# Low words of the weights and the residual, added by accumulating transfers instead of VectorE

## The chip, the cores and the metric

The kernel runs on one core of a Trainium2 chip. Its engines are TensorE (matrix products, in the profile PE, its weight loads PEld), VectorE (DVE), ScalarE (ACT), GpSimd (POOL) and SyncE (SP), which here only issues transfers. The metric is the device time of one execution in microseconds. Lower is better.

## The reference

There are 4 batches of 1088 positions, with 4 heads of 32 channels. The first part is an attention with a feature map instead of a softmax: two small projections a = S1 x and b = S2 x of 8 channels each, whose 64 products are the features.

```python
def phi(x):
    a = np.einsum('rd,bhsd->bhsr', S1, x)
    b = np.einsum('rd,bhsd->bhsr', S2, x)
    return np.einsum('bhsi,bhsj->bhsij', a, b).reshape(*x.shape[:-1], r * r)
q_p, k_p = phi(q), phi(k)
kv = np.einsum('bhsf,bhsd->bhfd', k_p, v)
z = np.sum(k_p, axis=2)
out = np.einsum('bhsf,bhfd->bhsd', q_p, kv) / (np.einsum('bhsf,bhf->bhs', q_p, z)[..., None] + 1e-6)
```

Its output, with the heads side by side, is x (4 x 1088 x 128). The second part is a gated feed-forward layer, in which a 1088 x 1088 matrix w_sg mixes the positions:

```python
h = gelu_tanh(x @ w_in)                # 128 -> 1024
u, v = h[..., :512], h[..., 512:]
v_n = (v - mean(v)) / sqrt(var(v) + 1e-6) * g_ln
v_s = np.einsum('ts,bsd->btd', w_sg, v_n) + b_sg[None, :, None]
return x + (u * v_s) @ w_out           # 512 -> 128, and the residual x
```

## The kernel before

**Words.** Most products run on float32r operands. An operand is split into a high word (its copy to float32r) and a low word (the operand less its high word), and a product is three matmuls: high with high, low with high, high with low. The names end in h and l: w_h and w_l are the words of w_sg, xh and xl those of x, ar holds both words of the normalised v, win, wout, gh/gl and kvt likewise. Line 806 makes the low words of w_sg: `V.tensor_sub(w_l[t][r], w_f[t][r], f32(w_h[r, t]))`, with w_f the loaded fp32 tile and w_h made from it by ScalarE (line 798).

**Tiles.** w_sg (transposed) lies in nine tiles of 128 input positions by 1088 output positions; the last has 64 rows. The outputs are taken in three chunks (CH) of 362, 362 and 364 columns. The 512 channels are four blocks (db) of 128. Tile t of w_l is put into the buffer of w_f tile t - 1, which must then have been read by all; the first has a spare one.

**The head** (class Head) does the attention of batch 0, its first layer, the normalisation and the mixing of its first channel block with unsplit fp32 weights (line 792), by an order written out in HEAD. Of its steps `wlo` is left out; the nine subtractions are tasks of the planner, each behind the last one.

**Behind the head** everything is a task of the class Plan: engine, assumed duration, what it reads and writes, which buffer it takes and frees, and, for TensorE, a position (`pos`). `late` is the time that the planner puts between the end of a task and the start of those that use it on another engine; a transfer of SP has a term for its size. Plan.order then lays the tasks out: always the task that can start first, among equals the one with the earliest due time, where due times come from TensorE's positions. The instructions are issued in this order, so each engine's queue, SP's and GpSimd's too, is worked through in an order fixed beforehand. UNITS, OUTS and SIDE hold the positions of the tasks that are not in the main line of matmuls.

**The stages.** After the head, batch 0's block 1 is mixed by two passes over the nine tiles, the first with w_h (lines 1348, 1350), the second with w_l (line 1346), while batch 1's attention (function attention) fills in. Blocks 2 and 3 follow (function standard). Batches 1 to 3 use a scheme with fewer products (function pair, lines 992 to 994 and 1003, 1004), which needs four weight combinations for the middle chunk. The function combine makes them once: it loads pieces of w_sg to tmp, adds and splits them on VectorE and ScalarE, and puts them into the DRAM buffer td; the plain words of tiles 4 to 7 go there too (lines 1029 and 1031, from w_h and w_l). The function stream loads them from td into w_h and w_l when they are due (lines 1064 and 1066).

**Transfers.** Nearly all are issued by SP, in the planner's order; a transfer that has to wait holds those behind it in the queue. The attention of a batch sends its projected q through the DRAM buffer dq (lines 1120, 1127, 1130) to spread it over partitions into ea and eb, loads k, v and q (1074, 1073, 1108), and VectorE multiplies ea with eb (line 1133).

**GpSimd** computes the inverse deviations of the normalisation (rest_g, lines 389 to 399), on which ScalarE waits to scale v (line 407), and fills a few constants, among them the lower half of the last w_l tile (line 805).

**The residual.** The function store closes a chunk of a batch: VectorE adds x's high word to the PSUM sum (line 960) and then x's low word (line 962), and SP stores the chunk (line 963). Batch 3 has a way of its own (line 958 and the function finish).

Of the kernel before, what the change touches and what calls it, by code (L numbers as in the profile page):

```python
# [9 lines left out]
F32 = mybir.dt.float32  # L10
F32R = mybir.dt.float32r
# [3 lines left out]
ALU = mybir.AluOpType  # L15
PSUM = bass.MemoryType.PSUM

B, H, S, D, R = 4, 4, 1088, 32, 8
P = 128
NT = 9  # L20
SP = NT * P
C = H * D
# [13 lines left out]
STARTS = (0.0, 96.0, 166.0, 236.0)  # L36
SIDE = [
    dict(
        k=[-69.5, -129.7, -258.62, 75.49, -16.81, -86.04, 99.22, -240.4, 467.74],
        m=[44.69, -2.17, -319.74, 128.68, -11.47, -380.37, -268.7, -327.69, -223.35],  # L40
        q=[-500.43, 26.57, 6.61],
        n=[-114.19, -31.31, 54.44, 107.92, 21.3, 18.55],
        v=[79.56, 57.62, 53.21, 95.41, 35.99, 315.99, 135.47, 134.1, 132.66],
    ),
    dict(
        k=[218.33, 108.5, 326.21, 556.29, 74.57, 349.63, 133.75, 142.17, 225.9],
        m=[152.43, 77.78, 138.8, 126.37, 195.45, 192.13, 317.54, 192.52, 217.9],
        q=[180.4, 148.25, 224.71],
        n=[84, 60.63, 131.2, 152.41, 137.24, 137.3],
        v=[281.37, 122.55, 229.64, 134.94, 133.73, 377.89, 212.58, 231.54, 221.6],  # L50
    ),
    dict(
        k=[713.88, 618.5, 144.7, 446.47, 381.41, 661.37, 485.59, 592.49, 451.01],
        m=[544.76, 607.03, 749.31, 502.75, 435.58, 443.92, 701.5, 703.57, 650.71],
        q=[226.39, 486.87, 752.47],
        n=[331.16, 423.26, 232.12, 454.36, 318.97, 567.45],
        v=[174.62, 186.57, 195.46, 166.87, 182.54, 154.59, 170.58, 189.58, 182.28],
    ),
]
UNITS = [  # L60
    [-875.2, 12.55, 557.21],
    [2.71, 22.55, -216.57],
    [18.91, -70.82, -27.37],
    [-13.89, 13.83, 7.58],
    [279.85, -10.36, 44.7],
    [94.74, -5.75, 123.14],
    [707.44, 198.02, 352.81],
    [-16.87, 201.58, -1.1],
    [-37.3, 24.54, -11.45],
    [11.79, 635.2, 58.72],  # L70
    [-11.47, 344.92, 228.92],
    [3.94, 15.41, -20.81],
    [341.58, 228.07, 273.13],
    [213.33, -23.55, 35.18],
    [28.54, -43.91, 111.65],
    [61.61, 4.4, 340.75],
]
OUTS = [
    [12.14, 10.35, 36.95],
    [30.29, -7.66, -11.46],  # L80
    [20.16, -4.85, 29.52],
    [31.06, 7.15, 8.98],
    [-4.83, 12.03, 9.94],
    [6.46, 68.4, 12.69],
    [531.54, 460.78, 293.13],
    [-11.57, 77.49, 47.42],
    [-31.49, 49.03, -30.53],
    [59.58, -26.68, -27.79],
    [986.46, 99.38, 1064.04],
    [211.11, 37.91, 512.89],  # L90
    [7.13, 23.51, 4.52],
    [197.69, 92.31, 345.68],
    [264.01, 186.46, 4.38],
    [1.55, 384.4, 4.5],
]
HEAD = [
# [20 lines left out]
def f32(ap):  # L117
    return ap.bitcast(F32)
# [14 lines left out]
class Plan:  # L133
# [9 lines left out]
    def add(self, eng, dur, f, r=(), w=(), take=(), free=(), pos=None, late=None, start=None, after=(), kb=0):  # L143
        n = len(self.tasks)
        take = dict(take)
        r, w = list(r), list(w) + list(take)
        deps = set(after)
        for k in r + w:
            if k in self.wrote:
                deps.add(self.wrote[k])  # L150
        for k in w:
            deps.update(self.read.pop(k, ()))
        for k in w:
            self.wrote[k] = n
        for k in r:
            if k not in w:
                self.read.setdefault(k, []).append(n)
        deps.discard(n)
        late = (2.3 + kb / 300 if eng == "SP" else self.LATE.get(eng, 0)) if late is None else late
        self.tasks.append(dict(eng=eng, dur=dur, f=f, deps=deps, take=take, free=list(free), pos=pos, late=late, start=start, kb=kb))  # L160
        return n
# [94 lines left out]
def tile_kernel(ctx: ExitStack, tc: tile.TileContext, qd, kd, vd, sd, wd, bd, wind, gd, woutd, identd, outd):  # L256
    nc = tc.nc
    mm = nc.tensor.matmul
    V, A, G = nc.vector, nc.scalar, nc.gpsimd
    load = nc.sync.dma_start  # L260

    cpool = ctx.enter_context(tc.tile_pool(name="const", bufs=1))
    dram = ctx.enter_context(tc.tile_pool(name="dram", bufs=1, space=bass.MemoryType.DRAM))
# [37 lines left out]
    wpool = Pool(ctx.enter_context(tc.tile_pool(name="w", bufs=1)), 1, w=NT + 1)  # L301
    w_f, w_l = {}, {}
# [159 lines left out]
    class Head:  # L462
# [7 lines left out]
        def load(self, name, ns, f, after=()):  # L470
            self.s.at(name, "SP", 0.47, f, after, late=-ns)
# [347 lines left out]
    def xtiles(b, xp):  # L819
        return [xp.tile([P, SP], F32R, name=f"x{b % 2}_{i}", tag=f"x{b % 2}_{i}") for i in "hl"]  # L820

    xp0 = ctx.enter_context(tc.tile_pool(name="x0", bufs=1))
    xs = [xtiles(0, xp0)]
    g = Gate(0, xs[0])
    with tc.tile_pool(name="stage", bufs=1) as stp:
        head = Head(Pool(stp, 1, wst=2, kb0=2, den=2, bst=2, nv=3, ny=3, nh=3, np=3), xs[0], g)
# [14 lines left out]
    pot = [None] * 3  # L841

    plan = Plan(dict(ps=3, gt=NG, u=NU, gh=NH, gl=NL))
    add, got = plan.add, plan.got
    dv = lambda n: 0.075 + n * 1.04e-3
    ac = lambda n: 0.09 + n * 0.83e-3
    pe = lambda n: 0.005 + n * 0.443e-3

    def load_(_, kb, f, **kw):
        return add("SP", 0.47, f, kb=kb, **kw)  # L850
# [13 lines left out]
    def gt(k):  # L864
        return gtt[plan.got[k]]
# [14 lines left out]

    for c in range(3):
        add(None, 0, None, w=[("po", c)], start=START["PE"])
    for t in range(NT):
        lo = add("V", 1.29, head.s.steps["wlo", t][2], w=[("w", t, c, 1) for c in range(3)], after=[lo] if t else [])
    done_lo = lo

    clock = [0.0]

# [9 lines left out]
    def unit(b, q):  # L898
        db, ci = q
        c0, cw = CH[ci]  # L900
        k = ("pu", b, q)
        xh, xl = xs[b % 2]

        def f():
            o, cs, ws = ps(k)[:, :cw], slice(c0, c0 + cw), slice(P * db, P * db + P)
            mm(o, lhsT=win_h[:, ws], rhs=xh[:, cs], start=True, stop=False)  # L906
            mm(o, lhsT=win_l[:, ws], rhs=xh[:, cs], start=False, stop=False)  # L907
            mm(o, lhsT=win_h[:, ws], rhs=xl[:, cs], start=False, stop=True)  # L908

        pemain(3 * pe(cw), f, UNITS[4 * b + db][ci], r=[("win",)] + [("x", b % 2, c) for c in range(3)], take={k: "ps"})  # L910
        u = ("u", b, q)
        add("A", 0.05 + ac(cw), lambda: A.activation(utt[plan.got[u]][:, :cw], ps(k)[:, :cw], AF.Gelu_apprx_tanh),  # L912
            r=[k], take={u: "u"}, free=[k])
# [38 lines left out]
    def store(b, ci):  # L952
        c0, cw = CH[ci]
        cs = slice(c0, c0 + cw)
        xh, xl = xs[b % 2]
        k = ("o", b, ci)
        if b == B - 1:
            add("V", 0.06 + dv(cw), lambda: V.tensor_add(gt(k)[:, :cw], pot[ci][:, :cw], xf(ci)[:, :cw]), r=[("po", ci), ("xf", ci)], take={k: "gt"})
        else:
            add("V", 0.06 + dv(cw), lambda: V.tensor_add(gt(k)[:, :cw], pot[ci][:, :cw], f32(xh[:, cs])),  # L960
                r=[("po", ci)] + [("x", b % 2, c) for c in range(3)], take={k: "gt"})
            add("V", dv(cw), lambda: V.tensor_add(gt(k)[:, :cw], gt(k)[:, :cw], f32(xl[:, cs])), r=[("x", b % 2, c) for c in range(3)], w=[k])
        load_("", 186, lambda: load(outd[b, :, cs], gt(k)[:, :cw]), r=[k], free=[k])


    def words(dst, q, key, r, n=512):
# [102 lines left out]
    def attention(b):  # L1069
        xh, xl = xs[b % 2]  # L1070
# [34 lines left out]
        for ci, (c0, cw) in enumerate(CA):  # L1105
            cs = slice(c0, c0 + cw)
# [56 lines left out]
            if ci == 2:  # L1163
                for x in (xh, xl):
                    add("V", dv(64), lambda x=x: V.tensor_copy(x[:, S:SP], f32(x[:, S - 64 : S])), w=[xk])

        g = gates[b] = Gate(b, xs[b % 2])
        waste = kpt[2].bitcast(mybir.dt.bfloat16)
        s1 = slot(b, 1)
# [130 lines left out]
    def xf(ci):  # L1300
        if "x" not in now:
            now["x"] = here("r0")
        return now["x"][:, ci] if ci < 2 else now["r2"]
# [23 lines left out]

    add("A", 0.1, lambda: A.mul(ng_col, g_col, -1.0), w=["ng"])
    add("G", 0.1, lambda: G.memset(now["r2"][:, 360:], 1.0), w=[("r", 2, 0), ("r", 2, 1)])

    unit(0, (1, 0))
    for ci in range(3):
# [4 lines left out]
    for i in range(2 * NT):  # L1337
        t, low = i % NT, i >= NT
        for ci in range(3):
            cw = CH[ci][1]  # L1340
# [11 lines left out]
            k = dict(take={"z12": "ps"}) if ci == 2 and i == 0 else dict(w=[zks[ci]])  # L1352
            pemain((1 if low or t == 8 else 2) * pe(cw), f, r=[("ar", t // 4) if t < 8 else ("rs", 0)] + [("w", t, ci, 1)] * low, **k)
        if i in (9, 11, 13):
            q = units.pop(0)
# [6 lines left out]
    for ci in range(3):  # L1362
        evac(0, (1, ci), zs[ci], zks[ci], g_col, free=["z12"] if ci == 2 else ())
        if ci:
            unit(0, (1, ci))
        gate(0, (1, ci))
    attention(1)
    for ci in (0, 1, 2):
        standard(0, 2, ci, ci % 2, (2, 3), 1)
# [11 lines left out]
    for b in range(1, B):  # L1381
        clock[0] = STARTS[b]
        if b == B - 1:
            before_end(b)
        pair(b, 0, e, zi)
        if b + 1 < B:
            attention(b + 1)
        pair(b, 1, e, 1 - zi)
# [38 lines left out]
```

## Time and profile before

| | |
|---|---|
| time, median of 3 runs | 348.51 us (346.77 to 349.98) |
| profiled execution | 347.09 us |
| its span, first to last instruction | 345.3 us |
| mean granted TensorE clock | 0.996 |
| busy PE / DVE / ACT / POOL | 332.4 / 271.4 / 217.7 / 23.0 us |
| moved by DMA | 68.87 MB, mean 199 GB/s |

A time is that of the whole execution; the span and all times of single instructions are those of the one profiled execution, counted from its first instruction. A row of a group of instructions gives line, engine, operation, output and inputs, shape, count, then busy us, mean ns of one, and the idle time of the engine ahead of them with what ended it. A row of waits gives who waited for whom, the total in us, how often, and the longest. The matmuls overlap, so TensorE counts as busy in gaps shorter than a matmul's own latency.

### The profile page before, as it was taken

Reading aid. Unit: us, or ns where it says so; the run is one execution under the profiler, and the core shown is the slowest. Engines: PE = TensorE matmul, PEld = TensorE weight load, DVE = VectorE, ACT = ScalarE, POOL = GpSimd, SP = SyncE. Lnnn points to the kernel's source line nnn. Section 1 sums busy time; section 2 is a strip of 40 time slices with the busy share of each in tenths; the row PEclk is TensorE's granted clock in tenths of the full one; section 3 lists DMA queues with packets and bytes.
Section 4 is the critical chain, followed back from the end, with each engine's and each line's share of the span. In section 5 each row is a group of like instructions: output and inputs, shape, how many; then the busy total and the mean of one; then the engine's idle time right before and its main releaser. Section 6 shows DMA issues by size and latency. Waiting matters only on the chain.

```text
span 345.3 us, 5940 instructions
## 1 busy us (share of the span) xinstructions
PE 332.4 (96%) x1952; PEld 311.4 (90%) x1952; DVE 271.4 (79%) x619; ACT 217.7 (63%) x517; POOL 23.0 (7%) x86
## 2 busy tenths in 40 slices
PE   8998999999999979999999999999999999999995
PEld 7876559998999869889999999999999999999994
DVE  4798999998997598979973989989647765874764
ACT  5476862464579989637659986658979644332331
POOL 0002000000000330000002400000006000000000
PEclk9999999999999999999999999999999999999998
DMA  7996033566567755899996854784509905874601
GB/s 246 392 393 219 7 104 99 151 203 192 164 189 253 211 158 151 269 276 325 265 282 196 271 153 132 210 284 152 172 19 317 348 7 173 289 272 136 210 26 62
DMA packets 56175, 68.87 MB, mean 199 GB/s; under 512 B 5008, under 2 KB 53456, under 8 KB 56144
## 3 DMA queue, kind: packets, MB, share of 16 engines
q1 hardware_dynamic: 56000, 68.40, 63.2%
q8 instruction: 15, 0.25, 0.3%
q14 instruction: 16, 0.13, 0.1%
q10 hardware_dynamic: 144, 0.09, 0.1%
HBM read 59.48 MB, written 8.99 MB: 198 GB/s over the span
## 4 chain that ended last, share of the span: by engine, by line
PE 70%; DMA 13%; DVE 11%; issue 2%; ACT 2%; SPq 1%; DVEq 0%
PE bz L992 12%; PE bz L993 11%; PE bz L994 11%; DMA eb<-dq 4%; DMA td<-tmp 3%; PE pz L792 3%; PE bs L1091 2%; PE pab L668 2%; DMA tmp<-in_w 2%; DMA w_h<-td 2%; PE bs L906 2%; PE bs L907 2%; PE bs L908 2%; PE bz L1004 2%; PE bz L1003 2%
## 5 line engine op out<-in xcount | busy, mean ns | idle before, releaser
L992 PE MATMUL bz<-w_h,ar 128*128 128x362 f32 (+1 forms) x288 | 95.6, 332 | 1.9 <-DMA w_h<-td 1.3
L993 PE MATMUL bz<-w_h,ar 128*128 128x362 f32 (+1 forms) x288 | 94.7, 329 | 0.2 <-DVE ar L968 0.2
L994 PE MATMUL bz<-w_l,ar 128*128 128x362 f32 (+1 forms) x288 | 94.7, 329 | 0.0
L992 PEld LDWEIGHTS bz<-w_h,ar 128*128 128x128 f32 x288 | 54.3, 188 | 3.7 <-DMA w_h<-td 1.7
L993 PEld LDWEIGHTS bz<-w_h,ar 128*128 128x128 f32 x288 | 54.2, 188 | 1.0 <-DVE ar L968 0.5
L994 PEld LDWEIGHTS bz<-w_l,ar 128*128 128x128 f32 x288 | 54.2, 188 | 0.0
L967 ACT CAST ar<-vn 128x512 fp32r<-128x512 f32 x40 | 24.7, 620 | 23.1 <-PE bz L994 21.9
L936 ACT CAST gh<-gt 128x362 fp32r<-128x362 f32 (+1 forms) x47 | 23.1, 496 | 21.7 <-DVE gt L935 10.9
L968 DVE TENSOR_TENSOR ar<-vn,ar 128x512 fp32r<-128x512 f32 x40 | 27.3, 684 | 8.0 <-ACT ar L967 7.8
L912 ACT ACTIVATE u<-bs 128x362 f32<-128x362 f32 (+1 forms) x48 | 22.4, 470 | 15.4 <-PE bs L908 7.6
L937 DVE TENSOR_TENSOR gl<-gt,gh 128x362 fp32r<-128x362 f32 (+1 forms) x47 | 24.6, 532 | 6.7 <-ACT gh L936 6.6
L407 ACT ACTIVATE vn<-vn,st 128x512 f32<-128x512 f32 x36 | 27.7, 815 | 2.9 <-POOL st L538 2.3
L935 DVE TENSOR_TENSOR gt<-gt,u 128x362 f32<-128x362 f32 (+1 forms) x47 | 24.5, 529 | 1.5 <-ACT u L912 1.1
L922 DVE SCALAR_TENSOR_TENSOR gt<-bz,g_col,b_bc 128x362 f32<-128x362 f32 (+1 forms) x31 | 18.0, 588 | 6.4 <-PE bz L1004 4.1
L1188 ACT ACTIVATE kp<-vn,st 128x512 bf16<-128x512 f32 x27 | 19.5, 721 | 0.2
L1091 PE MATMUL bs<-vx,kp 128*128 128x128 f32 x108 | 16.4, 276 | 1.7 <-DVE kp L335 1.7
L792 PE MATMUL pz<-w_f,vn 128*128 128x362 f32 (+3 forms) x54 | 17.6, 472 | 0.3 <-ACT vn L407 0.3
L1185 ACT ACTIVATE vn<-bs 128x512 f32<-128x512 f32 x27 | 15.9, 590 | 1.7 <-PE bs L1178 1.7
L946 PE MATMUL po<-gl,wout_h 128*128 128x362 f32 (+1 forms) x47 | 15.7, 334 | 0.9 <-DVE gl L937 0.8
L1091 PEld LDWEIGHTS bs<-vx,kp 128*128 128x128 f32 x108 | 14.6, 191 | 2.0 <-DVE kp L335 2.0
L906 PE MATMUL bs<-x_h,win_h 128*128 128x362 f32 (+1 forms) x48 | 16.4, 341 | 0.0
L907 PE MATMUL bs<-x_h,win_l 128*128 128x362 f32 (+1 forms) x48 | 15.7, 328 | 0.0
(273 smaller groups left out, 744.7 us busy)
## 6 DMA issues: line engine op xcount, KB each, us to landing
w_l<-td SPq DMA_DIRECT2D x96, 181.0 KB, 5.0
w_h<-td SPq DMA_DIRECT2D x48, 362.0 KB, 4.4
w_f<-in_w SPq DMA_DIRECT2D x9, 544.0 KB, 11.2
tmp<-in_w SPq DMA_DIRECT2D x16, 181.0 KB, 2.8
vx<-in_v SPq DMA_DIRECT2D x8, 288.0 KB
ea<-dq SPq DMA_DIRECT2D x12, 182.0 KB, 3.1
eb<-dq SPq DMA_DIRECT2D x12, 182.0 KB
td<-tmp SPq DMA_DIRECT2D x8, 271.5 KB, 3.7
```

The lines of the kernel that those rows point to most:

```text
L407: A.activation(self.vn(t), self.vn(t), AF.Identity, bias=self.nm[:, t : t + 1], scale=self.rs[:, t : t + 1])
L792: return mm(zs[ci], lhsT=vn[r, t, :P], rhs=w_f[t][r, c0 : c0 + cw], start=(t == 0), stop=(t == NT - 1),)
L906: mm(o, lhsT=win_h[:, ws], rhs=xh[:, cs], start=True, stop=False)
L935: add("V", dv(cw), lambda: V.tensor_mul(gt(k)[:, :cw], gt(k)[:, :cw], utt[plan.got[u]][:, :cw]), r=[u], w=[k], free=[u])
L936: add("A", ac(cw), lambda: A.copy(ght[plan.got[h]][:, :cw], gt(k)[:, :cw]), r=[k], take={h: "gh"})
L937: add("V", dv(cw), lambda: V.tensor_sub(glt[plan.got[l]][:, :cw], gt(k)[:, :cw], f32(ght[plan.got[h]][:, :cw])), r=[h, k], take={l: "gl"}, ...
L967: add("A", ac(n), lambda: A.copy(dst[:, 0], q()), r=r, w=[key])
L968: add("V", dv(n), lambda: V.tensor_sub(dst[:, 1], q(), f32(dst[:, 0])), r=r, w=[key])
L992: mm(o, lhsT=ar[e][:, 0, t], rhs=wh, start=first, stop=False, skip_group_check=True)
L993: mm(o, lhsT=ar[e][:, 1, t], rhs=wh, start=False, stop=False, skip_group_check=True)
L994: mm(o, lhsT=ar[e][:, 0, t], rhs=wl, start=False, stop=last, skip_group_check=True)
L1091: mm(ps(pkv)[:, P * p : P * p + P], lhsT=kpt[t % 3][:, P * p : P * p + P], rhs=vx[:, NT : NT + t + 2 : t + 1] if p else vx[:, t : NT + 1 : ...
```

## The change

1. **Low words of w_sg.** The nine subtractions on VectorE are gone. In their place ScalarE writes the negative of the tile to w_l, rounded to float32r (`A.mul(w_l, w_f, -1.0)`), which is the negative of the high word; then GpSimd issues a transfer that reads the tile of w_sg from DRAM once more and adds it to w_l in SBUF (`accum_op=ALU.add`). The planner assumes 1.2 us of GpSimd's time for an issue and 4.5 us until the result can be used. All that used w_l waits for that transfer. `done_lo`, behind which the fourth combination's buffer (t4a) may be filled, is now the last negation.
2. **Residual of batches 0 to 2.** A DRAM buffer od for each batch gets x's high word by a transfer of SP, to which one of GpSimd adds x's low word (function residual, called for batch 0 ahead of the first unit and for batches 1 and 2 at the end of their attention). For each chunk VectorE only copies the PSUM sum to SBUF, and GpSimd adds that to od by a transfer; after the third chunk SP copies od to the output.
3. **Order.** UNITS, OUTS and SIDE have new values. HEAD is the same.

```diff
     for t in range(NT):
-        lo = add("V", 1.29, head.s.steps["wlo", t][2], w=[("w", t, c, 1) for c in range(3)], after=[lo] if t else [])
-    done_lo = lo
+        neg = add("A", ac(S), lambda t=t: w_neg(t), w=[("w", t, c, 1) for c in range(3)], after=[neg] if t else [])
+        add("G", 1.2, lambda t=t: w_lo(t), w=[("w", t, c, 1) for c in range(3)], late=4.5)
+    done_lo = neg
...
+    def w_neg(t):
+        r = slice(0, P if t < NT - 1 else 64)
+        w_l[t] = wpool([P, S], "w", f"w_l{t}", F32R)
+        if t == NT - 1:
+            G.memset(f32(w_l[t][64:128]), 0.0)
+        A.mul(w_l[t][r], w_f[t][r], -1.0)
+
+    def w_lo(t):
+        r = slice(0, P if t < NT - 1 else 64)
+        G.dma_start(w_l[t][r], wd[r, t], accum_op=ALU.add)
...
         else:
-            add("V", 0.06 + dv(cw), lambda: V.tensor_add(gt(k)[:, :cw], pot[ci][:, :cw], f32(xh[:, cs])),
-                r=[("po", ci)] + [("x", b % 2, c) for c in range(3)], take={k: "gt"})
-            add("V", dv(cw), lambda: V.tensor_add(gt(k)[:, :cw], gt(k)[:, :cw], f32(xl[:, cs])), r=[("x", b % 2, c) for c in range(3)], w=[k])
+            add("V", 0.06 + dv(cw), lambda: V.tensor_copy(gt(k)[:, :cw], pot[ci][:, :cw]), r=[("po", ci)], take={k: "gt"})
+            add("G", 1.2, lambda: G.dma_start(od[b][:, cs], gt(k)[:, :cw], accum_op=ALU.add), r=[k], w=[("od", b)], free=[k], late=4.0)
+            stored.append((b, ci))
+            if len(stored) % 3 == 0:
+                load_("", 550, lambda: load(outd[b], od[b]), r=[("od", b)])
+            return
...
+    od = [dram.tile([C, S], F32, name=f"od{b}") for b in range(B - 1)]
+    stored = []
+
+    def residual(b):
+        xh, xl = xs[b % 2]
+        r = [("x", b % 2, c) for c in range(3)]
+        load_("", 550, lambda: load(od[b], f32(xh[:, :S])), r=r, w=[("od", b)])
+        add("G", 1.2, lambda: G.dma_start(od[b], f32(xl[:, :S]), accum_op=ALU.add), r=r, w=[("od", b)], late=4.0)
...
+        if b < B - 1:
+            residual(b)
         g = gates[b] = Gate(b, xs[b % 2])
...
+    residual(0)

     unit(0, (1, 0))
```

More of the change, by code (lines that the diff above doesn't have):

```diff
@@ L38 @@
     dict(
[L39 to L43, printed above, removed]
+        k=[-3.60834e+06, -9.45691e+06, -1.71359e+07, 9.72138e+06, -3714.23, -5.24817e+06, 6.95568e+06, -1.77702e+07, 3.65468e+07],
+        m=[6923.94, 7808.71, -6312.36, 13056.8, 7394.88, -11610, -7171.01, -7439.31, -3876.64],
+        q=[-682.24, -30.01, 9.82],
+        n=[-192.91, -23.96, 80.07, 448.58, 62.35, 60.57],
+        v=[109.06, 128.05, 72.55, 194.32, 30.51, 454.71, 213.62, 277.24, 218.16],
     ),
     dict(
[L46 to L50, printed above, removed]
+        k=[308.54, 50.13, 468.87, 974.67, 67.61, 496.34, 97.47, 211.16, 416.56],
+        m=[149.19, 141.94, 140.09, 232.36, 238.91, 219.41, 406.79, 278.21, 316.2],
+        q=[219.01, 97.54, 336.17],
+        n=[56.3, 85.49, 163.56, 146.42, 105.12, 197],
+        v=[377.39, 131.26, 381.09, 208.42, 206.87, 563.57, 336.01, 256.19, 290.58],
     ),
     dict(
[L53 to L57, printed above, removed]
+        k=[665.81, 706.39, 321.93, 639.07, 528.62, 616.52, 540.34, 856.15, 641.63],
+        m=[817.04, 1043.65, 1112.3, 739.16, 751.31, 638.5, 1014.71, 1060.34, 1034.91],
+        q=[346.47, 577.41, 595.04],
+        n=[168.42, 244.28, 274.58, 326, 332.1, 484.67],
+        v=[145.59, 154.24, 181.71, 178.62, 189.76, 191.76, 204.3, 142.14, 188.38],
     ),
@@ L60 @@
 UNITS = [
[L61 to L76, printed above, removed]
+    [-7469.96, -117.34, 6838.08],
+    [12.1, 29.71, -303.79],
+    [80.26, -253.43, -11.4],
+    [-31.36, 50.17, 9.87],
+    [262.83, -11.82, 271.64],
+    [171.72, -12.48, 225.52],
+    [1239.66, -14.17, 275.54],
+    [-97.32, 370.05, -59.5],
+    [-56.97, -30.83, -19.36],
+    [-39.45, 908.38, 1.38],
+    [199.84, 809.67, 835.33],
+    [54.35, 40.07, 390.74],
+    [426.74, 114.89, 746.14],
+    [51.73, -63.86, -33.99],
+    [236.75, -4.97, 221.39],
+    [109.29, 9.25, 486.08],
 ]
 OUTS = [
[L79 to L94, printed above, removed]
+    [33.47, 49.87, 56.06],
+    [97.89, 11.88, 8.43],
+    [14.61, 29.78, 70.97],
+    [57.45, 33.4, -4.3],
+    [-32.56, 10.96, -1.41],
+    [96.46, 176.51, 16.6],
+    [1114.36, 891.06, 201.48],
+    [-23.88, 231.02, 122.79],
+    [-1.7, 259.92, -30.54],
+    [54.47, -23.15, -30.55],
+    [1487.04, 255.5, 1517.9],
+    [276.6, 22.5, 686.44],
+    [-2.44, 7.66, -9.05],
+    [361.19, 374.89, 708.41],
+    [533.47, 383.22, 12.72],
+    [2.33, 503.34, 4.5],
 ]
```

## The prediction

> **What bounds the kernel now.** I read the page's head first, then the engines by stage, then the waits of TensorE, then the chain.
>
> ```profile
> span 345.3 us, 5940 instructions
> PE 332.4 (96%) x1952; PEld 311.4 (90%) x1952; DVE 271.4 (79%) x619; ACT 217.7 (63%) x517; POOL 23.0 (7%) x86
> ```
>
> TensorE is busy for 96% of the span, VectorE for 79%, GpSimd for 7%. The change takes work from VectorE, so what matters is where TensorE is idle because of VectorE. The table by stage (busy us of PE, PEld, DVE, ACT, POOL, then granted clock, DMA share and GB/s) answers that:
>
> ```profile
> 50.00:60.00 10.00, 10.00 (x69) 9.26 (x68) 9.45 (x16) 2.18 (x10) 0.00 (x0) 1.00 0.27 82
> 60.00:70.00 10.00, 10.00 (x68) 9.99 (x67) 9.71 (x17) 4.93 (x12) 1.01 (x1) 1.00 0.54 161
> 80.00:100.00 20.00, 19.17 (x111) 18.08 (x110) 18.90 (x46) 10.90 (x25) 0.00 (x0) 1.00 0.59 169
> 100.00:144.00 44.00, 41.11 (x248) 38.52 (x247) 36.22 (x95) 38.74 (x109) 6.20 (x22) 1.00 0.67 198
> 144.00:172.00 28.00, 26.74 (x157) 25.84 (x158) 25.01 (x50) 17.38 (x41) 0.00 (x0) 1.00 1.02 294
> 172.00:236.00 64.00, 63.59 (x392) 62.32 (x392) 51.92 (x114) 46.99 (x115) 6.44 (x22) 1.00 0.73 223
> 236.00:330.00 94.00, 94.00 (x557) 92.80 (x556) 64.48 (x128) 53.37 (x124) 6.37 (x22) 1.00 0.57 185
> ```
>
> Where the low words are made (50 to 70 us) VectorE is full, yet TensorE misses nothing. From 236 on TensorE misses nothing either. The idle time lies between: 0.83 in 80 to 100, 2.89 in 100 to 144, 1.26 in 144 to 172, 0.41 in 172 to 236, together 5.4 us. That is the ceiling of the gain behind the head, 1.6% of the span, since the change takes no matmul away. What ended these waits:
>
> ```profile
> PE bs L1091 <- DVE kp L335: 1.7, 1, 1.7
> PE bz L992 <- DMA w_h<-td: 1.3, 1, 1.3
> ...
> PE po L946 <- DVE gl L937: 0.8, 2, 0.4
> ...
> PE bs L1083 <- DVE kp L335: 0.7, 1, 0.7
> PE bz L992 <- DVE gt L922: 0.6, 2, 0.3
> ```
>
> VectorE ended 1.7 + 0.8 + 0.7 + 0.6 = 3.8 us of them and a transfer 1.3. But the two waits for kp have a transfer behind them, as the chain shows:
>
> ```profile
> 115.55 5.25 DMA eb<-dq
> 120.93 0.92 DVE ea L1133
> 121.84 0.67 DVE kp L335 x2
> ...
> 148.94 7.20 DMA w_h<-td
> ```
>
> VectorE stood waiting for eb before it came to kp, so those 2.4 us are a matter of the DMA. Sure to be VectorE's own are 0.8 + 0.6 = 1.4 us.
>
> **The low words: what goes, what comes.**
>
> ```profile
> L806 DVE TENSOR_TENSOR w_l<-w_f,w_h 128x1088 fp32r<-128x1088 f32 (+1 forms) x9 | 11.5, 1282 | 0.0
> ```
> ```profile
> L798 ACT CAST w_h<-w_f 128x1088 fp32r<-128x1088 f32 x9 | 9.8, 1101 | 3.8 <-DMA w_f<-in_w 3.8
> ```
>
> Nine subtractions leave VectorE, 11.5 us. ScalarE gets nine products of the same size; its nearest row, the copy of the same tile, gives 9 x 1.10 = 9.9 us. Their cover is ScalarE's idle time: from 50 to 70 it is busy for 2.18 + 4.93 of 20 us, so they cost nothing there except that a kb copy can stand up to 1.1 us behind one. GpSimd, busy for 1.01 us of these 20, has room for the issues (the planner in the code sets 1.2 us for each, 10.8 in all). Then come nine accumulating transfers, which no trace shows. Where the low words are made and read today:
>
> ```profile
> 34.52 1.28 DVE L806 TENSOR_TENSOR w_l<-w_f,w_h 128x1088 fp32r<-128x1088 f32 x1
> ```
> ```profile
> 52.20 1.28 DVE L806 TENSOR_TENSOR w_l<-w_f,w_h 128x1088 fp32r<-128x1088 f32 x1
> ...
> 68.83 1.28 DVE L806 TENSOR_TENSOR w_l<-w_f,w_h 64x1088 fp32r<-64x1088 f32 x1
> ```
> ```profile
> L1346 PE MATMUL bz<-w_l,ar x16: 322/326/412, 61.4 to 77.9; 128*128 128x362 f32 x16
> ...
> L1346 PE MATMUL bs<-w_l,rs x1: 328/328/328, 71.2 to 71.2; 128*128 128x364 f32 x1
> ```
>
> Tile 0 is made inside the head, tiles 1 to 8 from 52.2 to 70.1, and TensorE reads tile 8 at 71.2, 1.1 us after it is done. Low words that come later than 71.2 stop TensorE, whose order is fixed. The price of a transfer has these nearest rows:
>
> ```profile
> w_f<-in_w SPq DMA_DIRECT2D x9, 544.0 KB, 11.2
> ...
> out<-gt SPq DMA_DIRECT2D x8, 181.0 KB, 2.4
> ```
> ```profile
> 104.00:108.00 4.00, 4.00 (x23) 3.68 (x22) 3.36 (x10) 3.77 (x13) 0.00 (x0) 1.00 1.01 348
> ```
>
> A tile is 544 KB (557,056 bytes). With the engines full they moved 348 GB/s, so one plain pass takes 1.6 us. An accumulate must also read what it adds to; if that goes through the same engines, 3.2 us. Tiles 1 to 8 are 7.5 tiles (the last has half the rows), so 12 or 24 us from 52.2 on, and a landing of 2.4. Alone on the engines that ends at 66.6 or 78.6. SP's own transfers took 0.27 x 10 + 0.54 x 10 = 8.1 us in these 20; shared in full, the ends are 74.7 and 86.7. So tile 8 lands between 66.6, which would cost nothing and so excludes a gain of its own, and 86.7, 15.5 us after its first reader. I take the middle of the two inner values, 76.6, because SP's queue will hold part of its traffic back (next step): TensorE then waits 5.4 us, **+5**.
>
> ```profile
> 59.46 1.85 SPq L1031 DMA_DIRECT2D td<-w_l  x2
> 63.85 1.72 SPq L1073 DMA_DIRECT2D vx<-in_v  x2
> 65.66 0.38 SPq L1031 DMA_DIRECT2D td<-w_l  x1
> ...
> 68.68 0.32 SPq L1031 DMA_DIRECT2D td<-w_l  x1
> 69.09 0.67 SPq L1059 DMA_DIRECT2D td<-tmp  x1
> 69.94 0.50 SPq L1120 DMA_DIRECT2D dq<-ab  x1
> ```
>
> The copies of w_l tiles 4 to 7 to the td buffer stand in SP's queue, and each will wait for its accumulate. Behind them are the vx loads, tmp, and the dq and eb transfers of batch 1's attention, the very ones on the chain at 115 us. They move back with the low words. TensorE itself has moved back by 5 then, so only the remainder counts; I take **+1**, from nothing to the 0.83 us of idle in 80 to 100 doubled.
>
> For the doubled pass there is a rule. The Trainium skill (Collectives: The Full Stack, section "The bandwidth ceiling: the fold count and why AG ≠ RS ≠ AR") says that an add in the DMA engine costs no cycles, but has two source reads on the same ring, which halves the rate. No run here shows an accumulate; by that rule the upper price, 3.2 us, would hold and the sum would come to 360.5, as worked out for the second rival below.
>
> **The residual.**
>
> ```profile
> L960 DVE TENSOR_TENSOR gt<-po,x_h 128x362 f32<-128x362 f32 (+1 forms) x9 | 4.8, 529 | 0.8 <-PE po L946 0.7
> ...
> L962 DVE TENSOR_TENSOR gt<-gt,x_l 128x362 f32<-128x362 f32 (+1 forms) x9 | 4.7, 526 | 0.0
> ```
>
> Of two additions per chunk one goes (9 x 0.53 = 4.7 us) and one becomes a copy out of PSUM; no copy of that size from PSUM runs on VectorE today, so I leave it at 0.53, and at zero saving. Three a batch fall in stages where TensorE is not waiting (batches 1 and 2), so they give nothing there. In exchange each of three batches moves 544 KB to od, 544 KB added to it, three chunks of 181 KB added, and 544 KB from od to out, for three stores of 181 KB: 1,632 KB more. That of batch 0's input lies in the head's idle DMA time. The last copy of batch 0 falls where the transfers are full, at a share of 1.02 and 294 GB/s: 557 KB take 1.9 us there, and TensorE already waits 1.3 for a w_h that took 7.2 us to land (chain, above). I take **+1**, with 0 and 3 as ends (all its extra traffic there hidden, or the last chunk's two passes besides). For batches 1 and 2 the stages are at 0.73 and 0.57; there I put nothing, for the reason that TensorE waits 0.41 and 0.00.
>
> **The relief.** About 16 us less on VectorE, 10.3 of them in 52 to 70. Of the 5.4 us of idle I give back the sure 1.4 and a quarter of the kp waits (0.6): **-2**. Ends: 0 and -5.
>
> **Sum.** -2 + 5 + 1 + 1 = +5. The profiled execution took 347.1 (span 345.3 and 1.8 around it), so 352.1 on its scale. The median of the runs, 348.5, lies 1.4 above it; on that scale the forecast is 353.5. With the term of the low words between 2 and 9 its own range is 350.5 to 357.5. Below 345.0 or above 352.0 is a difference that a measurement tells from no change (1%).
>
> **Rivals.**
> *The transfers keep up (faster).* At 1.6 us a tile the end is 66.6 to 74.7, against 70.1 today. Then nothing is lost, and with VectorE free by 52 to 70 everything behind it moves up: 3.5 to 5 of the 5.4 us of idle return, 344. For it: TensorE's full rate elsewhere, DMA at 0.27 and 0.54. Against it: 1.3 + 2.4 us of that idle hang on transfers, and these get company.
> *Two reads in full.* Tile 8 lands at 86.7; TensorE stands for 15.5 us, wins back 4.5 of its later idle time meanwhile, and with the +1 comes to 360.5.
> *GpSimd's queue.* The normalisation runs on GpSimd, and an accumulate ahead of it waits there for the copy to od to land.
>
> ```profile
> 187.05 0.41 POOL L389 TENSOR_TENSOR st<-st 128x5 f32<-128x5 f32 x1 [59.09 <-DVE st L367]
> ```
>
> GpSimd is waiting for its input today, 59 us long. A landing of 2.4 to 11.2 us (rows above) ahead of it, once in each of three batches, half of it hidden by batch work that TensorE has: 3 x 0.5 x 4 = 6, so 354.5 without the stall of the low words. It decides from the point where the wait is longer than TensorE's other work in the plan.
> *Both are small.* The low words are late by under 3 us and the relief gives under 3: 347 to 350.
>
> **How the numbers follow.** Forecast 0.36, of which 0.08 below 352.0; transfers keep up 0.26; both small 0.20; two reads in full 0.10; GpSimd's queue 0.08. Slower by over 1%: 0.28 + 0.10 + 0.08 = 0.46. Within 1%: 0.20 + 0.08 = 0.28. Faster: 0.26. The range of 343.5 (all of -5) to 360.5 (two reads in full) leaves out about 0.15: the upper half of that rival and the ends of the two others.
>
> **What would show it.** Right: L1346, or whichever low matmul of tile 6 to 8 comes first, waits for a transfer into w_l, some 5 us in all, between 62 and 80; SP's td copies start later than 59.5 and 68.7; VectorE is busy for some 255 us. Wrong, on the fast side: the accumulates land 1.6 to 2 us apart, no wait of TensorE names w_l before 80, and the idle time from 80 to 172 is under 2 us. Wrong, on the slow side: landings over 3 us apart, or a gap in 107 to 130, 185 to 200 or 257 to 265 in which ScalarE's normalisation waits for GpSimd.

## The result and the profile after

The changed kernel takes 379.17 us (median of 4 runs, 375.04 to 381.4) against 348.50 for the kernel before: a ratio of 1.080, with a 95% interval of 1.070 to 1.091. The forecast was 353.5 with a range of 343.5 to 360.5, so the side was right and the size far off. Two of the four runs, the profiled one among them, lie more than 1.5% above the fastest, and the ratio, and every median, range and ratio below, leaves out such runs of a kernel: the changed kernel then stands at 376.3, so +28 us where +5 were expected. The profiled execution took 381.4, its span is 379.6.

The page's head, and from its third part the two large DMA queues (packets, MB, share of the 16 engines' span), of the changed kernel:

```profile
span 379.6 us, 5975 instructions
PE 341.3 (90%) x1952; PEld 317.3 (84%) x1952; DVE 256.5 (68%) x601; ACT 226.3 (60%) x526; POOL 40.2 (11%) x107
...
q1 hardware_dynamic: 55232, 70.07, 59.6%
q0 software_dynamic: 2960, 8.08, 11.7%
```

VectorE has lost 15 us of work, as the change meant, and TensorE's idle time has gone from 345.3 - 332.4 = 12.9 us to 38.3. The queue q0 carries what GpSimd issues. The stages of the changed kernel, in the columns of the prediction's table:

```profile
50.00:60.00 10.00, 10.00 (x46) 7.47 (x45) 8.63 (x20) 4.60 (x10) 6.45 (x7) 1.00 0.80 153
60.00:70.00 10.00, 4.50 (x33) 4.20 (x31) 0.42 (x1) 4.13 (x8) 3.59 (x4) 0.96 1.07 218
70.00:80.00 10.00, 0.00 (x0) 0.00 (x0) 0.00 (x0) 0.00 (x0) 0.00 (x0) 0.50 1.06 218
80.00:100.00 20.00, 15.79 (x90) 15.73 (x91) 12.72 (x30) 9.51 (x27) 0.00 (x0) 0.76 0.72 191
...
144.00:172.00 28.00, 25.64 (x157) 24.30 (x156) 22.98 (x54) 17.42 (x44) 0.87 (x5) 0.94 0.64 193
172.00:236.00 64.00, 59.86 (x348) 57.24 (x347) 45.49 (x97) 46.09 (x116) 10.82 (x27) 0.97 0.94 265
```

From 70 to 80 us no compute engine does anything. Only the DMA engines work, and they are full (a share of 1.06) while they move 218 GB/s; in the kernel before, full engines moved 348. The waits of the changed kernel say who stood where (total, times, longest):

```profile
DVE tmp L1069 <- DMA tmp<-in_w: 24.2, 4, 21.0
...
PE bs L1107 <- DVE kp L335: 19.7, 1, 19.7
POOL od L987 <- DVE wot L494: 18.8, 1, 18.8
```

TensorE's one long wait names kp, not a low word. The chain of the changed kernel (start, us, what) tells what stood behind kp:

```profile
56.90 11.16 DMA td<-tmp
...
68.07 15.38 DMA tmp<-in_w
...
83.47 0.35 DVE tmp L1069
83.82 0.34 DVE kp L335
...
84.21 0.81 PE bs L1107 x2
```

VectorE's queue had reached a subtraction of the function combine (L1069), which needs a piece of w_sg in tmp. That load, and the copy to td before it, took 15.4 and 11.2 us to land. In the kernel before, the same kinds landed in 2.8 and 4.1 us (issues from 30 to 90 us; KB each, median us to landing):

```profile
tmp<-in_w SPq DMA_DIRECT2D x4, 181.0 KB, 2.8
...
td<-tmp SPq DMA_DIRECT2D x3, 181.0 KB, 4.1
```

The kp products stood behind the subtraction. The timeline of GpSimd shows what filled the DMA engines meanwhile:

```profile
52.02 1.06 POOL L987 DMA_DIRECT2D od<-x_l  x1 [18.82 <-DVE wot L494]
52.82 5.66 POOL L892 DMA_DIRECT2D w_l<-in_w  x6
```

GpSimd had stood for 18.8 us at the addition of x's low word to od, which waits for the copy of x's high word; that copy was behind the 724 KB copy of w_h in SP's queue. (The row names VectorE; that the copy was what it waited for shows where the copy is issued earlier, under "Theory B, cleanly".) Low words whose negation was ready from 27 us on went out from 52.8 on, six in a row, and nine in all, 4.74 MB.

### The profile page after: what moved, and what is told of

Its sections match the earlier page's. It is cut to its first block, busy times and chain, and to the rows that moved or that the text cites. A ratio compares the mean times of both kernels' runs of the same rounds, so it can differ in the third digit from the quotient of the medians.

```text
span 379.6 us, 5975 instructions
## 1 busy us (share of the span) xinstructions
PE 341.3 (90%) x1952; PEld 317.3 (84%) x1952; DVE 256.5 (68%) x601; ACT 226.3 (60%) x526; POOL 40.2 (11%) x107
## 4 chain that ended last, share of the span: by engine, by line
PE 57%; DMA 24%; ACT 8%; DVE 5%; issue 3%; SPq 1%; DVEq 0%; ACTq 0%
PE bz L1016 10%; PE bz L1018 10%; PE bz L1017 10%; DMA td<-tmp 9%; DMA tmp<-in_w 7%; DMA eb<-dq 3%; PE bs L1115 2%; PE pab L668 2%; DMA w_l<-td 2%; PE bz L1028 1%; PE bz L1027 1%; PE po L958 1%; PE pz L792 1%; DMA w_h<-td 1%; PE po L956 1%
## 5 line engine op out<-in xcount | busy, mean ns | idle before, releaser
L1107 PE MATMUL bs<-sk,vn 128*128 128x128 f32 x54 | 11.2, 305 | 20.9 <-DVE kp L335 19.7
L1107 PEld LDWEIGHTS bs<-sk,vn 128*128 128x128 f32 x54 | 9.5, 211 | 22.5 <-DVE kp L335 20.3
L973 POOL DMA_DIRECT2D od<-gt x9 | 8.1, 1070 | 121.9 <-DVE gt L972 121.8
L1110 ACT COPY kb<-bs 128x32 f32<-128x32 f32 x27 | 4.8, 179 | 26.7 <-PE bs L1107 26.4
L792 PE MATMUL pz<-w_f,vn 128*128 128x362 f32 (+3 forms) x54 | 18.4, 485 | 2.2 <-ACT vn L407 2.2
L1069 DVE TENSOR_TENSOR tmp<-tmp 128x181 f32<-128x181 f32 x8 | 2.7, 343 | 24.2 <-DMA tmp<-in_w 24.2
## 6 DMA issues: line engine op xcount, KB each, us to landing
w_f<-in_w SPq DMA_DIRECT2D x9, 544.0 KB, 10.7
```

What stands on the lines that cost most here:

```text
L792: return mm(zs[ci], lhsT=vn[r, t, :P], rhs=w_f[t][r, c0 : c0 + cw], start=(t == 0), stop=(t == NT - 1),)
L1107: mm(ps(pk)[:, :P], lhsT=vn[:, t, 256 * s : 256 * s + P], rhs=sk, start=True, stop=True)
```

## The experiments

Three theories stood at the start. **A**: an accumulating transfer keeps all DMA engines busy for about 3 us a tile, so nine hold back everything else for some 27 us wherever they start. **B**: what matters is the head of GpSimd's queue, the od transfer that delays and bunches them. **C**: the new order costs by itself. A fourth, **D**, came with the first results: VectorE's in-order queue makes a late transfer of combine into a wait of TensorE. Each kernel was timed beside the kernel before, whose median was 347.0 to 348.3.

**Theory B, first try.** The od transfer of batch 0 is issued behind the nine low-word transfers.

```diff
-        add("G", 1.2, lambda: G.dma_start(od[b], f32(xl[:, :S]), accum_op=ALU.add), r=r,
+        f = lambda: G.dma_start(od[b], f32(xl[:, :S]), accum_op=ALU.add)
+        add("G", 1.2, f if b else lambda: held.append(f), r=r,      # held is issued after tile 8
```

> One GpSimd instruction moves: the transfer that adds batch 0's x_l to od goes behind the nine transfers of the low words instead of ahead of them. All else, every other engine's queue included, is that of the changed kernel (379.2 us). Theory B (GpSimd's queue): the low words of tiles 0 to 2, negated by ScalarE at 27 to 38 us, are held until 52.8 by that one transfer, whose input comes late; freed, they run while the DMA engines idle at 35 to 46, most of the 19.7 us wait of TensorE goes, and the time is 352 to 360. Theory A (the transfers are too heavy wherever they start: 3 us of all sixteen engines a tile): the stall only moves or shrinks by a few us, 370 to 379. Theory C (the new order itself costs): no change, 379.

Measured: 373.06 (369.91 to 375.19), ratio 1.073 (1.065 to 1.081). The gap shrank from 19.7 to 5.6 us, but a new wait came up in the head. The waits of TensorE and, below them, the timeline of GpSimd in this kernel:

```profile
PE pz L792 <- ACT vn L407: 6.0, 1, 6.0
PE bs L1112 <- DVE kp L335: 5.8, 2, 5.6
```
```profile
32.91 0.89 POOL L894 DMA_DIRECT2D w_l<-in_w  x1 [2.36 <-ACT w_l L890]
33.56 0.68 POOL L528 TENSOR_TENSOR nh<-nh,nv 128x3 f32<-128x3 f32 x1
36.98 0.88 POOL L894 DMA_DIRECT2D w_l<-in_w  x1 [2.74 <-ACT tmp L1080]
```

With the od transfer gone, low-word transfers were laid between the steps of the head's normalisation (L527 to L538), and each waited there for its negation (the last row names the ScalarE instruction right behind it); the last step ran at 40.4, not at 33.0. The time lies in A's range and not in B's, but the run changed two things, and its 3 us (376.3 to 373.1) are no clean price for B.

**The parts.** Three kernels keep the tasks and the order of the changed one and alter only what they emit. In the two that undo the residual, VectorE's additions of x read, in some chunks, the x of a later batch, since the order doesn't know of that reading; the work is the same.

```diff
 # residual undone (first and third kernel)
-   V.tensor_copy(gt, po); G.dma_start(od[b][:, cs], gt, accum_op=ALU.add); ... load(outd[b], od[b])
+   V.tensor_add(gt, po, xh); V.tensor_add(gt, gt, xl); load(outd[b, :, cs], gt)
 # low words undone (second and third kernel)
-   A.mul(w_l[t], w_f[t], -1.0); G.dma_start(w_l[t], wd[:, t], accum_op=ALU.add)
+   V.tensor_sub(w_l[t], w_f[t], f32(w_h[:, t]))
```

Residual undone, low words by transfers:

> The residual is added as before (two additions on VectorE, a store by SP for each chunk), with the low words by accumulating transfers and the order of the changed kernel. No od transfer is left, so nothing holds the low words back either. Theory B: 348 to 357, and against the run that only moves the od transfer the difference is what the rest of the residual's traffic costs, 0 to 5 us. Theory A: 365 to 375. Theory C: 375 or more.

Low words undone, residual by transfers:

> The low words are subtracted on VectorE again, at the place in the order where ScalarE's negations stood, and no transfer makes them; residual and order are those of the changed kernel. Theories A and B: the wait of 19.7 us goes, 347 to 355; what is left over 348.5 is the price of the residual's transfers and of the order. Theory C: 365 or more.

Both undone, the order alone:

> Both parts undone, so that the operations are those of the kernel before, issued in the order of the changed kernel: the order alone. Theories A and B: 346 to 351. Theory C: 365 or more, with a wait of TensorE near 64 us as in the changed kernel.

| kernel | us | ratio to before (95%) |
|---|---|---|
| changed | 376.34 | 1.080 (1.070 to 1.091) |
| residual undone | 367.00 | 1.052 (1.042 to 1.061) |
| low words undone | 359.10 | 1.030 (1.023 to 1.036) |
| order alone | 354.50 | 1.018 (1.011 to 1.025) |

Taken one after the other: the order 354.5 - 348.3 = 6.2, the residual 359.1 - 354.5 = 4.6 (the intervals leave some 1 to 8), the low words 376.3 - 359.1 = 17.2. Without the residual the low words come to 367.0 - 354.5 = 12.5; that kernel, too, has no od transfer ahead of them and shows the wait of 6.0 us in the head. The last two kernels lie between the ranges that were expected. Theory C holds in part: with the nine subtractions back on VectorE the new order is slower than the old one. TensorE then waits twice for kp, 2.1 and 2.0 us.

**Theory B, cleanly.** Two neighbours in SP's queue change places, so that the od transfer, and the low words behind it, can go earlier while GpSimd's own order stays.

```diff
-   load(td[3, :, 0], w_h[:, 4:8, 362:724]);  load(od[0], x_h)
+   load(od[0], x_h);  load(td[3, :, 0], w_h[:, 4:8, 362:724])
```

> The changed kernel with one pair of neighbours in SP's queue exchanged: the copy of x's high word to od of batch 0 is issued ahead of the 724 KB copy of w_h to td, not behind it. So od<-x_l, and with it the low-word transfers behind it in GpSimd's queue, can go from about 46 us and not from 52, while the order on GpSimd stays (the first of these experiments had also put low-word transfers between the steps of the head's normalisation). Theory B (the head of GpSimd's queue): the gap of 19.7 us shrinks by the 6 us gained, to 12 to 14, and the time to 370 to 373. Theory A (27 us of all DMA engines, wherever they start): the nine transfers then run from 46 to 76, the transfers of combine wait behind them as before, and the gap keeps 16 to 19 us, the time 375 to 379.

Measured: 373.00 (370.76 to 374.47), ratio 1.072 (1.066 to 1.079). GpSimd and TensorE in this kernel:

```profile
43.75 1.06 POOL L992 DMA_DIRECT2D od<-x_l  x1 [9.94 <-DMA od<-x_h]
44.55 2.98 POOL L892 DMA_DIRECT2D w_l<-in_w  x3
```
```profile
PE bs L1113 <- DVE kp L335: 12.5, 2, 12.3
```

The first low words went 8 us earlier, the gap shrank by 7, and the time lies in B's range. It fell by 3 us, which the intervals of the two kernels don't tell from nothing; a cleaner pair follows under theory D. The other 25 us above the kernel before are left: the queue's head is a part of the cause, not the cause.

**The price of the second pass.** The nine transfers load w_l and add nothing, so w_l holds w and not its low word.

```diff
-        G.dma_start(w_l[t][r], wd[r, t], accum_op=ALU.add)
+        G.dma_start(w_l[t][r], wd[r, t])
```

> The changed kernel with the nine low-word transfers as plain loads of the same size from the same place by the same queue, so that w_l holds w and not its low word; all else as it is. Theory A with two passes (the add reads what it adds to through the same engines): a tile takes 1.6 us and not 2.9, the nine are done by about 68 us and not 82, the gap of 19.7 us shrinks to 5 or less, and the time is 362 to 367. If GpSimd's queue is what is slow, whatever it carries, the tile still takes about 3 us and the time stays at 375 to 381.

Measured: 368.76 (366.35 to 369.58), ratio 1.059 (1.053 to 1.066). The same bytes by the same queue, without the add, in the table by stage, in TensorE's waits and in the chain:

```profile
60.00:70.00 10.00, 4.74 (x34) 4.44 (x32) 0.42 (x1) 4.13 (x8) 2.56 (x4) 0.97 1.11 387
```
```profile
PE bs L1107 <- DVE kp L335: 9.0, 1, 9.0
```
```profile
64.93 8.07 DMA tmp<-in_w
```

387 GB/s against the changed kernel's 218 in the same stretch, both with full engines. GpSimd's queue isn't slow; the add is. It is worth 376.3 - 368.8 = 7.6 us of the time and 10.7 of the gap. That is less than the 12 to 17 expected, since with nine plain loads combine's load still takes 8 us to land. At 387 GB/s a plain tile takes about 1.4 us, less than the prediction's lower price, and yet 368.8 - 359.1 = 9.7 of the 17.2 us of the low words are left: the larger part of their cost doesn't come from the add.

**Low words in the old order.** The kernel before, with negation and accumulating transfer at the place of each subtraction.

```diff
-        lo = add("V", 1.29, head.s.steps["wlo", t][2], ...
+        lo = add("V", 1.29, w_neg, ...      # A.mul(w_l, w_f, -1.0); G.dma_start(w_l, wd, accum_op=ALU.add)
```

> The kernel before, with its own order, and of the change only the low words: at the place of each subtraction ScalarE's negation and GpSimd's accumulating transfer are issued. No od stands ahead of them in GpSimd's queue, and the first of them meets idle DMA engines. Theory A: the transfers cost what they cost in the order of after, 13.3 us (367.8 less 354.5), so 360 to 363, and TensorE's wait again names kp or another result of VectorE. Theory D (VectorE's queue: what stops TensorE in the changed kernel is not a low word but the product of kp behind combine's additions, which the new order puts early): here the combine stands later, so TensorE stops at a low matmul that waits for a transfer into w_l, for 5 to 10 us, and the time is 352 to 357. The lone first transfer will show the price of one accumulate: 3 us or more by theory A, 1.6 us if the engines keep their 348 GB/s.

Measured: 371.03 (369.62 to 373.7), ratio 1.068 (1.062 to 1.074), 23 us slower. Its span is 369.9; the queue of GpSimd, which here carries only the nine tiles, the stretch in which the first of them meets idle DMA engines, and the waits:

```profile
q0 software_dynamic: 1232, 4.74, 7.1%
```
```profile
51.00:52.00 1.00, 1.00 (x8) 1.00 (x8) 0.51 (x2) 0.69 (x4) 0.00 (x0) 1.00 1.06 104
```
```profile
PE bs L1099 <- DVE kp L335: 10.0, 2, 8.3
PE bs L1354 <- DMA w_l<-in_w: 7.8, 1, 7.8
PE bz L1354 <- DMA w_l<-in_w: 3.2, 2, 2.8
```
```profile
ACT r L1142 <- DVE ea L1141: 21.1, 4, 13.8
DVE ea L1141 <- DMA eb<-dq: 19.9, 6, 12.4
```
```profile
POOL w_l L890 <- ACT w_l L889: 14.9, 1, 14.9
```

7.1% of 369.9 us is 26.3 us of all 16 engines for 8.5 full tiles, 3.1 us each, at 180 GB/s. From 51 to 52 us the first of them has the engines almost to itself and already fills them (a share of 1.06). TensorE stops both at low words (11.0 us) and at kp (10.0), there through VectorE, which stood for 12.4 us at the attention's product ea for a starved load of eb. Both kinds of wait are there, as A and D had them, and the time is above what either expected. The last rows show why: a negation stood in ScalarE's queue behind r, which waits for ea, so GpSimd waited 14.9 us for it, and the backlog delayed the very low words that were to follow.

**The residual in the old order.** x's words go to od when a batch's first channel block is evacuated; od goes out after the third chunk. In the first version the words of batches 1 and 2 were copied twice, in the second once.

```diff
-   V.tensor_add(gt, po, xh); V.tensor_add(gt, gt, xl); load(outd[b, :, cs], gt)
+   V.tensor_copy(gt, po); G.dma_start(od[b][:, cs], gt, accum_op=ALU.add); if third: load(outd[b], od[b])
```

> The kernel before, with its own order, and of the change only the residual of batches 0 to 2: x's words go to od when the batch's first channel block is evacuated, VectorE only copies the chunks, GpSimd adds them to od, and SP copies od to the output. VectorE has nine additions less. If the residual's transfers cost as in the order of after (359.1 less 354.5), 352 to 354. If that cost came from their place in that order, no more than 1 us: 347 to 350. If VectorE's relief is worth something, below 347.

> The kernel before, with its own order, and the residual of batches 0 to 2 by transfers, as in the experiment that took 363.4, but the copy of x's two words to od issued once a batch; there it was issued twice for batches 1 and 2, and the second stood in SP's queue for 7.5 us ahead of the w_h loads. If that queue was the cost, the waits of TensorE for w_h fall from 8.2 us to 1 to 3 and the time to 350 to 354, about the 4.6 us that the residual costs in the order of after. If it stays above 358, the residual's own transfers are heavier in this order than in that of after.

Measured: 363.18 (362.49 to 363.65), ratio 1.045, and 357.47 (355.09 to 360.2), ratio 1.029 (1.022 to 1.037). The wait of TensorE for w_h and the wait of SP's queue at the copy of od, in the second version:

```profile
PE bz L1012 <- DMA w_h<-td: 4.6, 3, 2.4
```
```profile
SPq L979 <- DMA od<-gt: 13.7, 3, 7.1
```

The copy of od waits in SP's queue for GpSimd's additions to land, up to 7.1 us, and the w_h loads wait behind it. Copying the words once takes 6 us off, and the waits for w_h fall from 8.2 to 4.6, but the time stays above the 350 to 354 expected. The residual costs 357.5 - 347.0 = 10.5 us there and about 4.6 in the order that was planned with it.

**Theory D.** One VectorE instruction of the changed kernel, the subtraction at which it stood, is issued 13 instructions later, right ahead of the piece's next subtraction and behind kp products.

```diff
 # piece (0, 1) of combine only
-   V.tensor_sub(s[:, 0], s[:, 1], s[:, 0])      # at its place
+                                                # issued right ahead of the next line
    V.tensor_sub(s[:, 1], s[:, 3], s[:, 1])
```

> The changed kernel with one instruction of VectorE moved: the first subtraction of combine's second piece, in front of which VectorE stood for 21 us while its tmp transfer starved, is issued right ahead of the piece's next subtraction, 14 instructions later, behind the kp products of batch 1. No transfer is taken away or moved. Theory D (VectorE's queue): TensorE no longer waits 19.7 us for kp; it goes on with the kp products and stops at low matmuls that wait for a transfer into w_l, 6 to 10 us in all until the last lands at about 82, so the time is 367 to 372. Theory A alone (the engines are full to 82, whoever waits): something else of VectorE's or the attention's transfers takes the wait over at once, and the time stays within 3 us of 379.

Measured: 379.29 (379.0 to 380.79), ratio 1.093 (1.089 to 1.098): no gain at all. The waits of TensorE and the chain in this kernel:

```profile
PE bs L1119 <- DVE kp L335: 10.6, 2, 9.3
PE bz L1377 <- DMA w_l<-in_w: 7.9, 4, 2.4
```
```profile
55.84 11.05 DMA td<-tmp
...
67.37 15.52 DMA dq<-ab
...
84.93 4.45 DMA eb<-dq
```

The one wait of 19.7 us falls apart into 7.9 us at low matmuls and 9.3 at kp, now behind ea, whose operand went through dq: 91 KB that took 15.5 us to land. D names rightly where the wait shows, and is wrong on what it costs. In both kernels something that TensorE needed was in the backlog while the engines were full.

Both moves together, the exchange in SP's queue and the held instruction:

> The last experiment's move of one VectorE instruction and the exchange of two neighbours in SP's queue (x's high word ahead of w_h) together. If the two causes are separate, their gains add: 6 us of the exchange and what the move alone gives, 361 to 367. If they are two names for one wait, the sum is hardly less than the better of the two, 367 to 371. By either theory it stays above the 359.1 of the order with subtractions on VectorE, since the nine transfers still take 27 us of all engines.

Measured: 372.13 (369.73 to 373.01), ratio 1.071 (1.066 to 1.076), a little above both ranges and next to the 373.0 of the exchange alone: the held instruction is worth nothing. Against the kernel with only that instruction held, the exchange is worth 379.3 - 372.1 = 7.2 us, and here the intervals lie apart. This is the cleanest price of the queue's head (theory B).

**Fewer tiles.** The low words of tiles 0 to 3 by transfers, of 4 to 8 by VectorE, in the changed kernel.

```diff
-        A.mul(w_l[t][r], w_f[t][r], -1.0)
+        if t < 4: A.mul(w_l[t][r], w_f[t][r], -1.0)      # and the transfer
+        else: V.tensor_sub(w_l[t][r], w_f[t][r], f32(w_h[r, t]))
```

> The changed kernel with the low words of tiles 0 to 3 by negation and transfer and those of tiles 4 to 8 by VectorE's subtraction; all else as it is. The last experiment but two showed that small transfers of SP (dq<-ab, 91 KB, 15.5 us to land) starve behind the nine tiles, and moving the waiting instruction changed nothing in the time. If the cost of the low words is that backlog, it depends on how long the engines are full and not on the bytes alone: four tiles with the copy to od ahead of them are through at about 66 (52.8 and 4 times 3 us), before dq<-ab is issued at 67 to 68, so no wait of 9 us or more is left, TensorE waits under 4 us for kp and the time is 360 to 364, near the 359.1 of all nine on VectorE. If every tile costs alike, 4/9 of the 20 us remain: 367 to 369.

Measured: 368.82 (366.65 to 370.27), ratio 1.057 (1.043 to 1.072). TensorE's wait and the chain:

```profile
PE bs L1111 <- DVE kp L335: 8.4, 2, 8.1
```
```profile
56.62 11.68 DMA td<-tmp
68.32 3.08 DMA tmp<-in_w
```

No threshold shows. Four tiles cost 368.8 - 359.1 = 9.7 us, nine cost 17.2, some 1.9 to 2.4 a tile. The copy to td landed at 68.3, 2 us later than the 66 at which the expectation had the tiles through; combine's load, issued then, landed in 3.1 us. Within the intervals, which are wide (some 5 us), the tiles cost alike, somewhat less than the 3.1 us that each keeps the engines.

## Why the prediction was wrong

**What held.** VectorE was to be busy for some 255 us: 256.5. The copies of w_l to td were to move behind 59.5 and 68.7: they went from 87.4 on. The ceiling of a gain, 5.4 us of idle, was never touched. The relief of -2 shows in no run, and none had it without the transfers, so its own size stays open.

**The price of a transfer.** The bounds were 1.6 and 3.2 us a tile; I took an end of the backlog at 76.6, the middle. Measured are 3.1, the upper bound. That the add slows the engines themselves shows in the kernel with plain loads: 387 GB/s against 218 with full engines. The rule quoted in the prediction (the Trainium skill, Collectives: The Full Stack, section "The bandwidth ceiling: the fold count and why AG ≠ RS ≠ AR") says, of a collective's reduce step, that the second source read halves the rate. The measured 218 / 387 = 0.56 agrees. The rival "two reads in full" (0.10) had the price right and gave 15.5 us of stall; the gap was 19.7. The rival "transfers keep up" (0.26) fell with the 1.6 us, and would have fallen with plain loads too, which still cost 9.7 us. This was the mis-sized term: 7.6 us of the time.

**Who pays for it.** Here the reasoning failed, not only a size. I asked when the last tile would land and charged TensorE with the difference to its first reader, adding SP's traffic to the tiles' time. I never turned that round: the same full engines delay SP's transfers. The step on SP's queue, +1, dealt with the order of issue alone and gave no transfer behind the tiles a longer landing. The landings went from 2.8 and 4.1 us in the profile before to 11 to 15 (td<-tmp 11.2, tmp<-in_w 15.4, and dq<-ab 15.5 in the kernel with the held instruction), each on the way to the next. The low-word stall that I forecast exists: 7.9 us where the held instruction uncovers it, against my 5.4. In the changed kernel a longer wait lies over it, and none of its long waits names w_l.

**GpSimd's queue.** I had its head blocked by a copy to od, but in front of the normalisation of batches 1 to 3, at 354.5. In the changed kernel it blocked the low words of batch 0, worth 7.2 us by the exchange in SP's queue with the instruction held. In front of the normalisation the mechanism does show in the first experiment, in the head, at 6.0 us.

**ScalarE's cover.** The negations took 10.0 us as forecast at 9.9. In the head TensorE waits 2.2 us for ScalarE's vn, 0.3 before and at most 1.1 with the subtractions on VectorE. Some 1 to 2 us, which I had at nothing.

**The residual.** I took +1, with 3 as the upper end, and nothing for batches 1 and 2. Measured 4.6 in the new order. I counted its bytes in one stage and not what its copy holds back in SP's queue, nor the batches behind: from 172 to 236 the DMA share rose to 0.94 and TensorE idles 4.1 of 64 us (0.4 before, though the stages have shifted by some 25 us).

**The order.** I never priced the replanned order. Alone it costs 6.2 us when VectorE still makes the low words. What it costs with VectorE relieved wasn't measured by itself, since it can't be had apart from the transfers; so 6.2 + 4.6 + 17.2 = 28.0 is a ledger in one sequence, not three independent prices.

**The clock.** I left it out. After the gap TensorE runs slower, as the 4 us stretches of the changed kernel show:

```profile
68.00:72.00 4.00, 0.00 (x0) 0.00 (x0) 0.00 (x0) 0.00 (x0) 0.00 (x0) 0.65 1.07 221
84.00:88.00 4.00, 3.79 (x16) 3.79 (x17) 2.35 (x6) 2.00 (x6) 0.00 (x0) 0.50 0.49 127
88.00:92.00 4.00, 4.00 (x26) 4.00 (x25) 2.67 (x7) 1.30 (x6) 0.00 (x0) 0.79 0.98 315
92.00:96.00 4.00, 4.00 (x28) 3.96 (x27) 4.00 (x11) 3.66 (x10) 0.00 (x0) 1.00 0.31 64
```

At 0.50 and 0.79 of its speed TensorE loses about 4 x 0.50 + 4 x 0.21 = 2.8 us of work behind the gap. That is an estimate from these rows; no run tried it alone.

What stays open is the rest behind the gap: how the remaining idle time of 144 to 236 us splits between the residual, the new order and the delays that the gap passed on.

## What to carry to other kernels

Price a transfer that adds at two passes over the DMA engines (0.56 of the plain rate here), and send the bill to all who use them: before moving arithmetic into transfers, list every transfer that is due while they run, and give each the length of the backlog as its landing time, not the landing in the profile before. Moving the instruction that was seen waiting showed only the next one in the same backlog; what helped was less time on the engines (the plain loads, the fewer tiles) or an earlier start. Expect little from relieving an engine that the bounding engine doesn't wait for, even where that engine is full: the 15 us taken off VectorE gained nothing that any run shows.

## What the hardware showed that was not expected

- An accumulating transfer of 544 KB from DRAM into SBUF takes 3.1 us of all 16 DMA engines (26.3 us for 8.5 tiles), some 180 GB/s; full engines moved 348 in the kernel before, 218 with these transfers in the changed one and 387 with plain loads in their place.
- Behind nine of them a small transfer waited about as long as the backlog lasted: 91 KB, issued at 67.4 us, took 15.5 us to land.
- The granted clock was 0.65 on the mean of 68 to 72 us (TensorE stopped at 64.5), 0.50 from then on, still 0.50 in 84 to 88 with TensorE busy for 3.79 of the 4 us, and 1.00 only from 92 on: full speed came back 4 to 8 us after TensorE resumed at 84.2.
